# A planned instruction order, a new load order and a relay by TensorE in a two-layer attention and FFN kernel on one core

## Chip, core and metric

The kernel runs on one core of a Trainium2 chip. The metric is the device time of one execution in microseconds (us). The kernel before takes 599.5 us (median of three runs, 598.34 to 600.8). Engines are named TensorE (PE in the profile, its weight loads PEld), VectorE (DVE), ScalarE (ACT), GpSimd (POOL) and SyncE (SP).

## The reference, cut to what matters

```python
def reference(x, wq, wk, wv, wo, beta, w1, w2):     # x [1, 2048, 640] bf16, 32 heads of 20, Dff 1728
    for _ in range(2):
        x = x + A(layernorm(x), wq, wk, wv, wo, beta)
        x = x + relu(layernorm(x) @ w1) @ w2
    return x
# A: four segments of 512 tokens. In each: causal softmax attention inside the segment, plus a read of a
# memory M (phi(q) @ M / (phi(q) @ z)); the two are mixed by sigmoid(beta); then M and z take in phi(k), v.
```

Two layers of four segments are eight pieces of work. Segments within a layer depend on each other only through the memory, and the FFN of a segment needs that segment alone. So the work of different segments may be interleaved freely.

## The kernel before

All instructions come from Python generators ("streams": scores, apply, key and query projection, relay, FFN and so on). A list scheduler walks through them with modelled durations, and each time it picks the operation that can start first; ties go to the lower "due". The picked order is then fixed on each engine, with semaphores between engines.

```python
key = (round(rank), st[2].due, n)                  # earliest start, then due, then stream number
...
each(relay, "relay", -1.9, -1.8, 8)                # dues set by hand: segment number + an offset
each(out_proj, "oproj", -0.9, -0.8, 48)
each(ffn, "ffn", 1.4, 2.4, 220)
```

Scores are made in 160 rounds, 20 per segment. A round fills two pairs of PSUM banks with scores of four heads side by side (four row groups of the array), ScalarE takes two exponentials of 128x1024 from them, GpSimd masks. Each group of heads is then applied to the values in four column groups. In segment 0 the two pairs of banks are worked separately ("half-banks").

Heads have 20 columns, and 32 heads do not fit evenly into blocks of 128. The projections give five blocks; the rest sits in spare lanes and is brought to its place (`kqL`, groups 5 to 7) by a "relay" through DRAM, eight transfers per segment:

```python
def relay(a, s):
    ...
    for r in range(4):     # kqA -> scr (DRAM), one semaphore each
        ... dma("sp", scw_sem[z][r], 122880, f, ev)
    for r in range(4):     # scr (DRAM) -> kqL
        ... dma("sp", scr_sem[r], 122880, f, [wr[r]])
```

The loads at the start:

```python
def loads_sp():
    for i in (0, 2): yield from x0("sp", i)
    yield from ld("sp", "wk", 819200, ...)
    yield from ld("sp", "wq", 819200, ...)
    yield from ld("sp", "wv", 819200, ...)
def loads_act():
    for i in (1, 3): yield from x0("act", i)
    tb = yield dma("act", sem_("d_beta"), 16384, ...)   # beta to all 128 partitions
```

Where the plan sees a gap on TensorE, it puts useless 128-column matmuls of the identity into it ("fillers").

The softmax here doesn't subtract the row's maximum and nothing guards it: scores larger than these inputs give would overflow.

Of the kernel before, what the change touches and what calls it, by code (L numbers as in the profile page):

```python
# [1 line left out]

# [3 lines left out]
dt = mybir.dt  # L6
# [5 lines left out]
H = 32  # L12
# [145 lines left out]
HOT = 1.0  # L158

# [10 lines left out]
class Sched:  # L170
    def __init__(self, prog):
        self.P = prog
        self.free = {e: 0.0 for e in ENGS}
        self.t = {}
        self.events = {}
        self.streams = []
        self.dma_free = 0.0
        self.mode = "full"
        self.log = []
        self.now = -1.0  # L180
        self.fill = None
# [16 lines left out]
    def add(self, gen, name):  # L198
        self.streams.append([0, gen, None, None, False, name])
# [8 lines left out]
    def _settle(self, st):  # L208
        while not st[4]:
            if st[2] is None:  # L210
                try:
                    y = next(st[1]) if st[3] is None else st[1].send(st[3][0])
                except StopIteration:
                    st[4] = True
                    return False
                st[3] = None
                st[2] = y
            y = st[2]
            if isinstance(y, Op):
                return True  # L220
            if y.key not in self.events:
                return False
            st[2], st[3] = None, (self.events[y.key],)
        return False
# [38 lines left out]
    def _filled(self, start, mode):  # L263
# [17 lines left out]
        self.log.append(("pe", free, end, "fill", [], tk, n))  # L281
        self.mode = "full"

    def run(self):
        while True:
# [18 lines left out]
            for n, st in enumerate(self.streams):  # L304
# [6 lines left out]
                key = (round(rank), st[2].due, n)  # L311
# [43 lines left out]
            self.log.append((e, start, end, st[5], waits, out, len(fns)))  # L355
            st[2], st[3] = None, ((out, *got) if got else out,)

# [47 lines left out]
def bass_interleave_layers__memory_aug_infini_attn__dense_activation_relu__prompt_kernel(  # L405
    nc, A_x, A_wq, A_wk, A_wv, A_wo, A_beta, B_x, B_w1, B_w2, out,
):
    with contextlib.ExitStack() as es:
        sb = lambda name, shape, dtype=dt.bfloat16: es.enter_context(nc.sbuf_tensor(name, shape, dtype))
        sem_ = lambda name: es.enter_context(nc.semaphore(name))  # L410
        P = Prog({e: sem_("clk_" + e) for e in ["act", "dve", "pool", "pe"]})
        S = Sched(P)
# [6 lines left out]
        HALVES = (0,)  # L419
        NXT, NXN, NET = 3, 2, 2  # L420
# [50 lines left out]
        X = [Slot(ps[:, 0:2, :], "SX")]  # L471
        Y = [Slot(ps[:, 2:4, :], "SY")]
        OD = [Slot(ps[:, 4, :], "OD")]
        MISC = [Slot(ps[:, 5 + k, :], "misc%d" % k) for k in range(3)]
        XNT = [[Slot(k, "xnT") for k in range(2)], [Slot(2, "xnT")]]
        XN = [Slot(xn_tok[:, k], "xn") for k in range(NXN)]
        ST6 = [Slot(stats6[:, k], "st6") for k in range(4)]
        KQA = [[Slot(kqA[b][:, :, c], "kqA") for c in range(5)] for b in range(3)]
        KQL = [Slot(kqL, "kqL")]
        SCR = [[Slot(b, "scr")] for b in range(2)]  # L480
        VA = [[Slot(v_aug[k], "va")] for k in range(3)]
        PTS = [[Slot(PT[:, k], "pt")] for k in range(2)]
        PHQ = [Slot(phq, "phq")]
        KTK = [Slot(ktok, "ktok")]
        ET = [Slot(etmp[:, k], "et") for k in range(NET)]
        BDS = [[Slot(BD[:, 4 * h:4 * h + 4], "bd")] for h in range(2)]
        OSB = [[Slot(o_sb[:, k], "osb")] for k in range(2)]
        ORAW = [Slot(oraw[:, k], "oraw") for k in range(2)]
        OTOK = [Slot(k, "otok") for k in range(2)]
        RDEN = [Slot(rden[:, k], "rden") for k in range(2)]  # L490
        RMEM = [Slot(rmem[:, k], "rmem") for k in range(2)]
        OT = [Slot(oT[:, k], "oT") for k in range(2)]
        HT = [Slot(hT, "hT")]
        xnt_sem = [[sem_("xt%d_%d" % (k, i)) for i in range(NJ)] for k in range(NXT)]
        scw_sem = [[sem_("sw%d_%d" % (b, r)) for r in range(4)] for b in range(2)]
        scr_sem = [sem_("sr%d" % r) for r in range(4)]
        ktk_sem = [sem_("kt%d" % k) for k in range(3)]
        tok_sem = [sem_("tk%d" % k) for k in range(2)]
        ot_sem = [sem_("ot%d" % k) for k in range(2)]
        dout = [sem_("do%d" % k) for k in range(4)]  # L500

        def room(a, s):
            k = a * NSEG + s
            return 0 if k == 0 else 1 + (k - 1) % 2

        def kq(b, g, n):
            return kqA[b][:, n, g, :] if g < 5 else kqL[:, n, g - 5, :]

        def bf(bank):
            return bank.bitcast(dt.bfloat16)  # L510
# [3 lines left out]
        def ld(e, name, nbytes, fn, key, waits=(), issue=700.0):  # L514
            tk = yield dma(e, sem_("d_" + name), nbytes, fn, waits, issue=issue, rate=250.0)
            S.set(*key, v=[tk])
            return tk

        xs = A_x[0].rearrange("(t p) d -> p t d", p=128)

        def w_src(w):
            return w.rearrange("(c p) d -> p c d", p=128)

        def x0(e, i):
            yield from ld(e, "x0%d" % i, 163840, lambda e: e.dma_start(x_sb[:, i, :], xs[:, i, :]), ("x", 0, i))

        def loads_sp():
            for i in (0, 2):
                yield from x0("sp", i)
            yield from ld("sp", "wk", 819200, lambda e: e.dma_start(raw[0], w_src(A_wk)), ("wkr",))  # L530
            yield from ld("sp", "wq", 819200, lambda e: e.dma_start(raw[1], w_src(A_wq)), ("wqr",))
            yield from ld("sp", "wv", 819200, lambda e: e.dma_start(wv_r[:], w_src(A_wv)), ("wv",))

        def loads_act():
            for i in (1, 3):
                yield from x0("act", i)
            tb = yield dma("act", sem_("d_beta"), 16384, lambda e: e.dma_start(
                beta_bc[:], bass.AP(tensor=A_beta.tensor, offset=A_beta.offset, ap=[[0, 128], [1, H]])), lat=4000.0)
            S.set("beta", v=[tb])

        def loads_pool():
            def late(name, nbytes, fn, waits):
                tk = yield dma("pool", sem_("d_" + name), nbytes, fn, waits, issue=1100.0, rate=250.0,
                               lat=1700.0 + nbytes / 250.0)
                return tk

            def x(s, w):
                tk = yield from late("xs%d" % s, 655360, lambda e: e.dma_start(
                    x_sb[:, 4 * s:4 * s + 4, :], xs[:, 4 * s:4 * s + 4, :]), w)
                for i in range(4):  # L550
                    S.set("x", s, i, v=[tk])
                return [tk]

            w = yield Need("wv")
            w = yield from x(1, w)
            w = yield from x(2, w)
            w = yield from late("wo", 819200, lambda e: e.dma_start(wo_r[:], w_src(A_wo)), w)
            w = [w]
            S.set("wo", v=w)
            z1 = yield Need("z1")  # L560
            got = []
            for k in range(FC):
                tk = yield from late("w1%d" % k, 442368, lambda e, k=k: e.dma_start(
                    w1_r[:, k, 0:DFF], B_w1[128 * k:128 * k + 128, :]), z1 + w)
                got.append(tk)
                w = [tk]
            S.set("w1", v=got)
            w = yield from x(3, w)
            hold = KQA[0] + VA[0]
            yield Op([("pool", 0.0, 0.0, lambda: [])], [], hold=hold)  # L570
            w = w + [t for s in hold for t in s.old]
            got = []
            for k in range(4):
                c0, c1 = (0, 4, 8, 11, 13)[k], (0, 4, 8, 11, 13)[k + 1]
                tk = yield from late("w2%d" % k, 163840 * (c1 - c0), lambda e, c0=c0, c1=c1: e.dma_start(
                    w2_r[:, c0:c1, :], B_w2[128 * c0:128 * c1, :].rearrange("(c p) d -> p c d", p=128)), w)
                got.append(tk)
                w = [tk]
            tk = yield from late("w24", 81920, lambda e: e.dma_start(
                w2_r[0:DFF - NFULL * 128, NFULL, :], B_w2[NFULL * 128:DFF, :]), w)  # L580
            S.set("w2", v=got + [tk])

        def permute():
            got = []

            def part(n, c, src, w):
                dst = (wk_p, wq_p)[n][:, :, c * 128:(c + 1) * 128].rearrange("p k (r d) -> p k r d", r=4)
                tks = []
                for d0, d1, s0 in ((0, 20, 20 * c), (20, 32, 100 + 12 * c)):
                    o, i, m = dst[:, :, :, d0:d1], src[:, :, :, s0:s0 + d1 - d0], 20 * (d1 - d0)  # L590
# [11 lines left out]
            for c in range(FC):  # L602
                for n in range(2):
                    S.spawn(part(n, c, *ws[n]), "perm")
# [804 lines left out]
```

## Time and profile before

| | before |
|---|---|
| time, median | 599.5 us |
| span of the profiled run | 595.8 us |
| TensorE busy | 574.2 us, 96% |
| VectorE, ScalarE, GpSimd busy | 421.5, 429.1, 220.2 us |
| first scores | 19.9 us |
| round 20, round 40 of scores | 72.0, 124.6 us |
| last matmul ends | 593.0 us |

The lines are shown in the prediction below. TensorE's busy share hides gaps (the 512-column matmuls of L778 are recorded with 0.38 us each, though 13 in a row take 2.81 us, 0.216 each), so starts must be compared. I call **work** the sum of all matmuls at the start-to-start times that the prediction reads from the trace (a quarter for each of four side by side), plus 0.10 us for each change between the full array and the row or column groups. What the elapsed time has beyond it I call **holes**: waits, half clock (stretches in which the trace shows half the TensorE clock granted: 0.50 from 106.1 to 112.9 us in the kernel before) and smaller losses. The trace is cut at the last score matmuls of every ten rounds (called round 10, round 20 and so on), and for each piece both numbers are read. That shows where holes lie, which a share over the whole span does not.

### The profile page before, as it was taken

The page shows a single profiled execution, that of the slowest core. Times are in us where ns is not written, and L with a number is a line of the kernel's source. Part 1 is how long each engine was busy: PE and PEld are TensorE (multiplying, and loading weights), DVE is VectorE, ACT ScalarE, POOL GpSimd, SP SyncE. Part 2 cuts the span into 40 slices and gives each one's busy share as a digit, 9 for nine tenths or more (in the row PEclk, how much of TensorE's full clock was granted, in tenths as well). Part 3 has the DMA queues.
Part 4 walks back from the last instruction along what each step waited for, and adds up shares of the span by engine and source line. Part 5 has one row for each costly group of instructions (what it writes and reads, how often), then busy time and mean ns, then how long its engine had stood idle before and what let it go on. Part 6 is the DMA issues. An engine that isn't in the chain of part 4 may idle for free.

```text
span 595.8 us, 12451 instructions
## 1 busy us (share of the span) xinstructions
PE 574.2 (96%) x5099; PEld 298.8 (50%) x5099; DVE 421.5 (71%) x998; ACT 429.1 (72%) x523; POOL 220.2 (37%) x345
## 2 busy tenths in 40 slices
PE   8999998889999999999999999999999999999998
PEld 4444444334555444554444554455544654655655
DVE  5687579998799955999575971699828796744202
ACT  4879998899897998968786876979677687223140
POOL 5563545654353533435332440344322343002000
PEclk9999999799999999999999999999999999999999
DMA  6369743656818423146227521645304641522201
GB/s 210 96 140 181 143 105 48 157 109 125 95 18 137 86 53 61 31 100 119 52 49 102 73 47 21 70 91 111 72 1 70 119 101 20 102 67 23 67 0 45
DMA packets 127657, 49.42 MB, mean 83 GB/s; under 512 B 114144, under 2 KB 126304, under 8 KB 127600
## 3 DMA queue, kind: packets, MB, share of 16 engines
q1 hardware_dynamic: 125648, 41.08, 39.1%
q0 software_dynamic: 1520, 7.21, 4.2%
q8 instruction: 40, 0.66, 0.5%
q10 hardware_dynamic: 432, 0.34, 0.2%
q14 instruction: 17, 0.14, 0.1%
HBM read 14.26 MB, written 6.55 MB: 35 GB/s over the span
## 4 chain that ended last, share of the span: by engine, by line
PE 69%; DVE 15%; ACT 8%; DMA 5%; POOL 1%; issue 1%; SPq 0%; DVEq 0%
PE ps L1302 15%; PE ps L1322 15%; PE ps L778 13%; PE ps L1041 7%; PE ps L812 6%; PE ps L1254 6%; ACT PT L1055 5%; PE ps L1123 5%; DMA otok<-oraw 2%; DMA wb<-in_A_wk_dram 1%; DVE xn_tok L726 1%; DVE x_sb L1196 1%; DVE hT L1285 1%; DVE o_sb L980 1%; DVE otok L1167 1%; DVE ktok L897 1%
## 5 line engine op out<-in xcount | busy, mean ns | idle before, releaser
L1055 ACT ACTIVATE PT<-ps 128x1024 bf16<-128x1024 f32 x256 | 247.4, 1026 | 44.7 <-PE ps L1041 44.2
L1031 POOL TENSOR_SCALAR_AFFINE_SELECT PT<-PT 128x512 bf16<-128x512 bf16 x256 | 174.3, 698 | 271.0 <-ACT PT L1055 224.4
L1302 PE MATMUL ps<-xnT,wb 128*128 128x512 bf16 x560 | 134.8, 381 | 0.1
L1322 PE MATMUL ps<-wb,hT 128*128 128x320 bf16 x896 | 131.8, 299 | 2.8 <-ACT hT L1286 1.8
L1322 PEld LDWEIGHTS ps<-wb,hT 128*128 128x128 bf16 x896 | 83.4, 98 | 41.1 <-issue 5.8
L1196 DVE TENSOR_TENSOR x_sb<-x_sb,ps 128x320 bf16<-128x320 bf16 x128 | 60.8, 479 | 59.7 <-PE ps L1322 44.8
L1302 PEld LDWEIGHTS ps<-xnT,wb 128*128 128x128 bf16 x560 | 51.2, 98 | 60.6 <-issue 8.4
L1286 ACT ACTIVATE hT<-ps 128x512 bf16<-128x512 f32 x63 | 37.7, 601 | 56.3 <-PE ps L1302 56.2
L1052 ACT ACTIVATE PT<-ps 128x1024 bf16<-128x1024 f32 x64 | 62.0, 1022 | 19.8 <-PE ps L1041 19.5
L812 PE MATMUL ps<-wv_r,xnT 128*128 128x320 bf16 x320 | 68.8, 300 | 0.0
L778 PE MATMUL ps<-xnT,wk_p 128*128 128x512 bf16 x200 | 58.0, 380 | 0.4 <-DVE kq L765 0.4
L778 PE MATMUL ps<-xnT,wq_p 128*128 128x512 bf16 x200 | 57.2, 380 | 0.1
L1254 PE MATMUL ps<-wo_r,oT 128*128 128x320 bf16 x320 | 51.1, 300 | 2.7 <-DVE oT L1218 0.9
L765 DVE CAST kq<-ps 128x512 bf16<-128x512 f32 x41 | 28.1, 688 | 35.7 <-PE ps L778 35.4
L812 PEld LDWEIGHTS ps<-wv_r,xnT 128*128 128x128 bf16 x320 | 30.1, 98 | 23.6 <-issue 5.7
L1123 PE MATMUL ps<-PT,va 128*32 128x128 bf16 (+3 forms) x896 | 41.3, 305 | 0.0
L1254 PEld LDWEIGHTS ps<-wo_r,oT 128*128 128x128 bf16 x320 | 28.8, 98 | 21.0 <-issue 5.2
L1285 DVE TENSOR_SCALAR hT<-ps 128x512 bf16<-128x512 f32 x49 | 33.3, 679 | 8.1 <-PE ps L1302 7.9
L1041 PE MATMUL ps<-kq 20*128 20x512 bf16 (+3 forms) x560 | 35.3, 301 | 3.4 <-ACT PT L1055 2.3
L726 DVE TENSOR_SCALAR xn_tok<-x_sb,mv,rstd 128x640 bf16<-128x640 bf16 x64 | 34.5, 552 | 4.4 <-POOL rstd L722 3.2
L713 DVE BATCH_NORM_STATS2 stats<-x_sb 128x6 f32<-128x320 bf16 x64 | 29.4, 461 | 2.9 <-DMA x_sb<-in_A_x_dram 2.7
L714 DVE BATCH_NORM_STATS2 stats<-x_sb 128x6 f32<-128x320 bf16 x64 | 30.2, 471 | 0.0
(95 smaller groups left out, 603.0 us busy)
## 6 DMA issues: line engine op xcount, KB each, us to landing
kqL<-kq_scr SPq DMA_DIRECT2D x32, 120.0 KB
kq_scr<-kq SPq DMA_DIRECT2D x28, 120.0 KB
out_dram<-x_sb SPq DMA_DIRECT2D x16, 160.0 KB, 1.9
wb<-in_B_w_dram POOLq DMA_DIRECT2D x5, 432.0 KB, 4.7
x_sb<-in_A_x_dram POOLq DMA_DIRECT2D x3, 640.0 KB, 4.8
wb<-in_B_w_dram POOLq DMA_DIRECT2D x2, 640.0 KB, 4.9
xnT<-xn_tok SPq DMA_TRANSPOSE x52, 2.7
wb<-in_A_wk_dram SPq DMA_DIRECT2D x1, 800.0 KB, 8.4
```

Source lines behind the costliest of these rows:

```text
L726: tn, bx = yield dve(D, 4, lambda e, a, t=t: e.tensor_scalar(a, x_sb[:, t, :], mv[:, t, 0:1], rstd[:, t:t + 1], ALU.subtract, ALU.mult), [ ...
L778: fn = lambda e, bank, k=k, w_p=w_p, c=c: e.matmul(bank, w_p[:, k, c * 128:(c + 1) * 128], xnT[:, k_, :, k, :], start=(k == 0), stop=(k == ...
L812: fn = lambda e, bank, k=k, i=i, hf=hf: e.matmul(bank[:, 0:320], xnT[:, k_, i, k, :], wv_r[:, k, hf * 320:(hf + 1) * 320], start=(k == 0), ...
L1031: tm = yield pool(590.0, lambda e: e.affine_select(out=reg, in_=reg, pattern=[[0, 4], [1, 128]], compare_op=ALU.is_ge, fill=0.0, base=0, c ...
L1041: fns.append((lambda e, x=x, j=j, hh=hh, N=N, o=o: e.matmul(ps[:, hh, o:o + N], kq(b, gg[x], 0)[32 * hh:32 * hh + DH, 128 * j:128 * j + 12 ...
L1052: fn = lambda e: e.activation(PT[:, :, 2 * k:2 * k + 2, 1024:1280], bs.ap.rearrange("p h (x t) -> p x h t", x=2), ACT.Exp, scale=SCALE)
L1055: fn = lambda e: e.activation(PT[:, items[0], 2 * k:2 * k + 2, c0:c0 + 512], bs.ap, ACT.Exp, scale=SCALE)
L1123: return [(lambda e, hh=hh, j=j: e.matmul(bank[32 * hh:32 * hh + 32, 128 * j:L], v_flat[b][:, (j * H + 8 * hh + g) * E1:(j * H + 8 * hh + ...
L1196: ta = yield dve(320, 1, lambda e: e.tensor_tensor(xa, xa, bk.ap[:, 0:320], ALU.add), [tk], early=HOT)
L1254: fn = lambda e, bank, k=k, hf=hf, o=ot.ap: e.matmul(bank[:, 0:320], o[:, k, :], wo_r[:, k, hf * 320:(hf + 1) * 320], start=(k == 0), stop ...
L1302: fn = lambda e, bank, k=k, dc=dc: e.matmul(bank, w1_r[:, k, dc * 128:(dc + 1) * 128], xnT[:, k_, :, k, :], start=(k == 0), stop=(k == FC ...
L1322: fn = lambda e, bank, dc=dc, i=i, hf=hf: e.matmul(bank[:, 0:320], hTv[:, dc, i * 128:(i + 1) * 128], w2_r[:, dc, hf * 320:(hf + 1) * 320] ...
```

## The change

The intent is threefold. The order is planned in 20 passes: after each pass a backward sweep over the finished plan computes how late each operation could start, and these times are the dues of the next pass; the best pass is kept. wv is loaded ahead of wk and wq, since value projections need no permuted weights, and beta comes last. The first relay is done on TensorE: the identity's columns, copied into seven selection matrices, move the spare lanes to their place.

```diff
+def justify(S, dues, n):          # backward sweep: latest start of each op that keeps the end
+    ...                           # consumers + semaphore time, stream order, engine order
-            key = (round(rank), st[2].due, n)
+            key = (round(max(rank, self.free[e] + WIN[e])), st[2].due, n)      # WIN is 0 for all
...
-            yield from ld("sp", "wv", 819200, ...)          # after wk and wq
+            yield from ld("sp", "wv", 819200, ...)          # before wk and wq
...
+                w = yield Need("wqr")
                 tb = yield dma("act", sem_("d_beta"), 16384, ..., w, lat=4000.0)
...
+            def relay_pe(a, s):                             # only for the first segment of all
+                tz = yield dve(128 * len(pieces), 4, lambda e: e.memset(sel, 0.0))
+                for i, (m, c, d0, d1) in enumerate(pieces): # 7 column copies of the identity
+                    tk = yield dve(4 * (d1 - d0), 1, lambda e, ...: e.tensor_copy(...))
+                for m in range(3):
+                    for n in range(2):                      # keys, queries: 14 matmuls of 512 columns
+                        ... e.matmul(bank, sel[:, i], kqA[b][:, n, c, :], start=..., stop=...)
+                        S.spawn(out(m, n, bk, tk), "relay") # evacuation to kqL
...
-        each(relay, "relay", -1.9, -1.8, 8)
+            each(relay, "relay", -1.9, -1.8, 8, FIRST)      # hand dues of pass 0: first segment ahead
...
+        for n in range(PLANS):                              # PLANS = 20
+            P, S = plan(dues)
+            end = max(S.t.values())
+            if best is None or end < best[0]:
+                best = (end, P, S)
+            dues = justify(S, dues, n)
```

Cut: the bookkeeping of operation keys, the waits of the values for the ones columns that stand beside them (now only their readers wait), the model's constants for the first loads. The hand-set dues of pass 0 are not quite those of before: for the first segment the relay, the turning of its outputs, the output projection and the second layernorm are set 10 lower.

## The prediction

> **What bounds the kernel now.** I read the page first (busy shares, then the slices), then the windows by stage, the start in the timeline, and the chain of waits where the windows showed a hole. From the page:
>
> ```profile
> PE 574.2 (96%) x5099; PEld 298.8 (50%) x5099; DVE 421.5 (71%) x998; ACT 429.1 (72%) x523; POOL 220.2 (37%) x345
> ...
> PEclk9999999799999999999999999999999999999999
> ...
> PE 69%; DVE 15%; ACT 8%; DMA 5%; POOL 1%; issue 1%; SPq 0%; DVEq 0%
> ```
>
> TensorE is busy 96% of the span and carries 69% of the last chain, so the end is set by TensorE's work plus its holes. But its busy time is too kind: matmul records overlap. Starts give the true cost. In the timeline, a run of 13 512-column projections takes 2.81 us (0.216 each), ten 320-column ones 1.36 us (0.136 each); one 84-column matmul takes about 0.037, one 128-column 0.056; and a change between the full array and the four-row-group scores or the four-column-group applications adds 0.10 us: a lone value matmul before scores holds TensorE 0.23 instead of 0.136.
>
> I multiplied these into the instruction order of the kernel before: 960 x 0.216 + 1536 x 0.136 + 384 x 0.037 + 157 x 0.056 + 68 for scores and applications (160 rounds and 64 groups, four matmuls side by side) + 415 mode changes x 0.10 = about 552 us with the 14 warm-up matmuls. The last matmul ends at 593, so **about 41 us are holes**: that is all an order can win. Where they are, by windows (columns: length, then busy time of PE, PEld, DVE, ACT, POOL; clock; DMA share; GB/s):
>
> ```profile
> 44.00:72.00 28.00, 27.89 (x242) 11.86 (x242) 18.87 (x35) 25.93 (x32) 12.94 (x22) 1.00 0.80 152
> 72.00:97.00 25.00, 22.61 (x235) 10.89 (x232) 19.16 (x45) 22.57 (x27) 12.38 (x18) 1.00 0.59 115
> 97.00:125.00 28.00, 23.62 (x255) 10.92 (x256) 27.32 (x70) 24.74 (x29) 18.22 (x30) 0.88 0.52 115
> 125.00:153.00 28.00, 27.02 (x247) 11.54 (x243) 24.51 (x49) 25.49 (x30) 12.77 (x19) 1.00 0.56 106
> ...
> 500.00:594.00 94.00, 92.05 (x628) 56.12 (x620) 37.23 (x100) 24.60 (x41) 5.79 (x12) 1.00 0.22 47
> ```
>
> From 72 to 125 us TensorE is only 85 to 90% busy: there VectorE (27.3 of 28 us) and ScalarE are as full as it, and in the same window the granted clock falls (0.88). From 500 us on it runs alone and nearly without holes. In the hole the chain of waits goes through the exponentials in pairs, 2.4 to 2.8 us a round though two exponentials take only 1.9: the next scores need both banks, then a mode change.
>
> ```profile
> 90.63 1.84 ACT PT L1055 x2
> 92.47 0.05 issue
> 92.51 0.45 PE ps L1041 x8
> 92.96 1.93 ACT PT L1052 x2
> 94.89 0.05 issue
> 94.94 0.45 PE ps L1041 x4
> 95.39 1.92 ACT PT L1055 x2
> ```
>
> The start (timeline of TensorE): nothing useful before 12.5 us, with fillers (L622).
>
> ```profile
> 11.12 0.45 PE L690 MATMUL ps<-ident,xn_tok 128*128 128x128 bf16 x5 [1.69 <-DVE xn_tok L726]
> 11.41 1.28 PE L622 MATMUL ps<-ident 128*128 128x128 bf16 x20
> 12.53 1.24 PE L778 MATMUL ps<-xnT,wk_p 128*128 128x512 bf16 x5
> ```
>
> [...]the clock is halved in one stretch of 6.8 us, about 104 to 111 us, inside the thinnest window; that costs about 3.4 us.[...]the first relay's eight transfers through DRAM[...] queue on SyncE behind other issues (writes from 35 us, reads issued at 45.7, first use 56.8).
>
> **The change part by part.**
> 1. *Loads.* Issue to landing was 8.4, 10.1 and 11.6 us from 1.7, 2.2 and 2.8, so the three weight slots land near 10.1, 12.3 and 14.4. They now hold wv, wk, wq. The listing puts 18 value matmuls (2.4 us) between the first transposes and the first key matmul and drops 27 fillers (1.5 us). But keys wait for wk at 12.3 plus 0.5 of permuting, queries for wq at 14.4 plus 0.5: K at 12.9 to 14.0, a hole to 15.0, Q, K, Q, then three more key matmuls: 15.0 + 3.2 + 0.9 = first scores at 19.1 against 19.9. Win: 0.7 us, and 0.7 us of value work done ahead: about 1.5.
> 2. *Relay by TensorE.* Adds 14 matmuls of 512 columns (3.0 us) and, on VectorE and ScalarE, a clear, seven copies and six evacuations (about 5 us beside other work); removes eight transfers. The before-kernel never waits for that relay visibly, because the rounds had not come to it. It is needed so that rounds 12 to 20 may come early.
> 3. *Order.* Total issue work is then 552 + 3.0 - 1.5 + 13 more mode changes x 0.10 = 554.7. So the change raises the bound by 2.8 us and can win only by removing holes. I cut both listings at every tenth round of scores. Work of TensorE before / after in us, rounds 0-10: 21.4/19.5; 10-20: 25.5/17.5; 20-30: 22.2/25.8; 30-40: 19.0/22.5; actual time before: 24.5, 27.7, 25.5, 27.1. In the first twenty rounds (half-banks, whose two halves also cost TensorE some 2 us more per ten) ScalarE now has 22.2 and 20.2 us (20 exponentials x 0.915, plus the other instructions listed between them), so I give these 23.5 and 21.5; then 27.8 and 26.5, since ten paired rounds hold at least 24.5 plus a part of ScalarE's other work. Round 40 comes at 19.2 + 23.5 + 21.5 + 27.8 + 26.5 = 118.5, not 124.6: 6.1 us earlier. But by then 3.6 us less TensorE work is done (98.6 against 102.2). **Net 2.5 us** of the early holes and of the half clock.
> 4. *The rest.* 456.1 us of work are left, against 449.7 with 18.6 us of holes before. If holes stay: 118.5 + 456.1 + 18.6 = 593.2, nothing won. Ten-round stretches where TensorE has under 27 us are limited by the paired rounds to about 27.3; before had five such after round 40, after has three or four: 1 to 3 us. The others are waits over 0.15 us (12.8 of the 18.6): score to FFN, memory read for its phi, second FFN half for the last relu. Dues that know the distance to the end should help those, but many come from transfers and evacuations later than planned, which no plan sees. I take 3 to 4 us: last matmul at 589.5, time 3.5 earlier, plus something for a better draw than my floors: 594.
>
> **The rivals.**
> - *The plan closes most holes.* If half the 25 us of real waits goes, less 2.8 of new work: about 589; two thirds: 585. For it: holes are 41 us against 552, and the old priorities were ordinals by stage, not distances to the end. Against: holes are spread thin, about 1.4 us per 28.
> - *VectorE takes over as the bound.* Its work from rounds 20 to 30 grows from 18.3 to 29.3 us by the listing, more than the stretch lasts. Then TensorE waits there for evacuations, and the win of the first twenty rounds is handed back: 598 to 600.
> - *Merely moved slack.* ScalarE limits rounds 10 to 20, TensorE idles there and the half clock comes at another place: 600 to 602.
> - *The head is hidden.* The wait for wq turns the gain of part 1 to nothing: 1.5 us worse than my number.
>
> **Range and chances.** Centre 594.0 us: 599.5 less 2.5 less 3 to 4, rounded up for the gain in part 1 already counted. Low 586 is the first rival with half to two thirds of the waits gone; high 602 is moved slack. Faster by over 2% needs under 587.5, 12 us of 41 us of holes after paying 2.8: 0.20. Slower by over 2% would need new holes of 12 us in a plan that picks its best pass: 0.03. Same: 0.77.
>
> **What would show it.** First value matmul near 10.2, first key near 12.9, first scores near 19.1; exponentials of rounds 10 to 20 back to back and TensorE under 92% busy there; round 20 near 64 us; windows of 27 to 28 us per ten rounds from round 20 on; the half-clock stretch gone or moved; 14 new matmuls with 3 us; last 94 us as before. The prediction is wrong if the windows after 125 us show TensorE with clearly fewer holes than 1.4 us in 28 (then it is faster), or if VectorE is full between 64 and 95 us and TensorE waits for it (then there is no gain).

## The result and the profile after

The changed kernel takes **590.66 us** (median of four, 589.81 to 592.7) against 598.92 (four runs of the kernel before). The ratio is **0.9868** (95% interval 0.9826 to 0.9909). Ratios are the mean time of one kernel's fast runs over that of the other's in the same rounds, so not quite the ratio of the medians. A second measurement in five rounds gave 590.77 us and 0.9846 (0.983 to 0.9862). The kernel is faster by 1.3 to 1.5%: inside the stated range, within the 2% called "same", below the stated centre of 594.

The page of the profiled run (592.7 us, the slowest of its four):

```profile
PE 575.2 (97%) x5086; PEld 297.3 (50%) x5086; DVE 425.9 (72%) x1018; ACT 427.3 (72%) x520; POOL 215.5 (36%) x342
...
PEclk9979999999999999999999999999999999999999
...
PE 76%; DVE 13%; ACT 6%; DMA 3%; issue 1%; POOL 0%; SPq 0%
```

TensorE has 1 us more busy time in 5 us less span, and its share of the last chain rises from 69 to 76%. The slice with the low clock is now the third, not the eighth.

Windows by stage (length, then busy time of PE, PEld, DVE, ACT, POOL; clock; DMA share; GB/s):

```profile
44.00:72.00 28.00, 27.59 (x254) 10.18 (x256) 23.32 (x48) 27.06 (x31) 16.88 (x27) 1.00 0.53 107
72.00:97.00 25.00, 24.25 (x238) 11.63 (x228) 19.09 (x38) 23.20 (x30) 11.12 (x17) 1.00 0.71 127
97.00:125.00 28.00, 26.53 (x283) 12.88 (x280) 27.68 (x73) 26.15 (x32) 18.00 (x29) 1.00 0.55 88
125.00:153.00 28.00, 26.63 (x247) 11.99 (x248) 26.93 (x60) 23.74 (x27) 12.05 (x18) 1.00 0.71 144
...
500.00:588.00 88.00, 88.00 (x596) 54.62 (x594) 32.52 (x87) 19.70 (x33) 4.57 (x10) 1.00 0.22 47
```

The hole from 72 to 125 us has shrunk: TensorE 24.25 of 25 and 26.53 of 28 instead of 22.61 and 23.62. From 44 to 72 us ScalarE is busy 27.06 of 28 instead of 25.93. The chain of waits there consisted of exponentials before; now other TensorE work lies between the rounds (output projection L1418, key projection L878):

```profile
101.48 1.08 PE ps L878 x5
102.56 0.68 PE ps L1418 x5
103.24 0.38 PE ps L1205 x4
103.62 1.93 ACT PT L1219 x2
```

The start (timeline of TensorE; L912 are the values, L790 the transposes, L878 the keys):

```profile
9.00 0.57 PE L912 MATMUL ps<-wv_r,xnT 128*128 128x320 bf16 x3
9.41 0.44 PE L790 MATMUL ps<-ident,xn_tok 128*128 128x128 bf16 x5
...
12.22 0.58 PE L912 MATMUL ps<-wv_r,xnT 128*128 128x320 bf16 x3 [0.44 <-DVE wb L900]
12.63 1.24 PE L878 MATMUL ps<-xnT,wk_p 128*128 128x512 bf16 x5
```

The two traces cut at the rounds of scores (us; the estimate is the prediction's):

| point | before | after, estimated | after, measured | work up to there, before / after |
|---|---|---|---|---|
| first scores | 19.9 | 19.2 | 18.0 | 14.0 / 13.1 |
| round 10 | 44.4 | 42.7 | 45.3 | 35.5 / 32.8 |
| round 20 | 72.0 | 64.2 | 64.9 | 61.0 / 50.3 |
| round 30 | 97.5 | 92.0 | 92.9 | 83.2 / 76.1 |
| round 40 | 124.6 | 118.5 | 118.2 | 102.2 / 98.6 |
| last matmul | 593.0 | 589.5 | 588.1 | 551.9 / 554.7 |

Work is up by 2.8 us, holes are down from 41.1 to 33.4: from 22.4 to 19.6 up to round 40, and from 18.7 to 13.9 after it. That is the 4.9 us between the two last matmuls.

### The profile page after: what moved, and what is told of

Its sections match the earlier page's. It is cut to its first block, busy times and chain, and to the rows that moved or that the text cites.

```text
span 591.0 us, 12433 instructions
## 1 busy us (share of the span) xinstructions
PE 575.2 (97%) x5086; PEld 297.3 (50%) x5086; DVE 425.9 (72%) x1018; ACT 427.3 (72%) x520; POOL 215.5 (36%) x342
## 4 chain that ended last, share of the span: by engine, by line
PE 76%; DVE 13%; ACT 6%; DMA 3%; issue 1%; POOL 0%; SPq 0%
PE ps L1486 20%; PE ps L1466 16%; PE ps L878 13%; PE ps L1418 7%; PE ps L1205 7%; PE ps L1287 6%; PE ps L912 5%; ACT PT L1219 4%; DMA wb<-in_A_wk_dram 2%; DVE hT L1449 1%; ACT PT L1216 1%; DVE xn_tok L826 1%; DVE o_sb L1336 1%; PE ps L1155 1%; DMA oT<-o_sb 1%; DVE o_sb L1144 1%
## 5 line engine op out<-in xcount | busy, mean ns | idle before, releaser
L1195 POOL TENSOR_SCALAR_AFFINE_SELECT PT<-PT 128x512 bf16<-128x512 bf16 x256 | 172.2, 689 | 266.3 <-ACT PT L1219 220.1
L1450 ACT ACTIVATE hT<-ps 128x512 bf16<-128x512 f32 x54 | 32.3, 598 | 56.8 <-PE ps L1466 56.5
L1216 ACT ACTIVATE PT<-ps 128x1024 bf16<-128x1024 f32 x64 | 62.2, 1028 | 10.9 <-PE ps L1205 10.7
L912 PE MATMUL ps<-wv_r,xnT 128*128 128x320 bf16 x320 | 60.3, 300 | 1.5 <-DVE va L900 0.6
L865 DVE CAST kq<-ps 128x512 bf16<-128x512 f32 x44 | 30.1, 686 | 36.4 <-PE ps L878 36.4
L878 PE MATMUL ps<-xnT,wk_p 128*128 128x512 bf16 x200 | 55.3, 381 | 0.0
L878 PE MATMUL ps<-xnT,wq_p 128*128 128x512 bf16 x200 | 54.8, 386 | 0.1
L1418 PE MATMUL ps<-wo_r,oT 128*128 128x320 bf16 x320 | 52.6, 300 | 1.2 <-DMA oT<-o_sb 0.9
L1449 DVE TENSOR_SCALAR hT<-ps 128x512 bf16<-128x512 f32 x58 | 39.4, 681 | 8.2 <-PE ps L1466 7.7
L912 PEld LDWEIGHTS ps<-wv_r,xnT 128*128 128x128 bf16 x320 | 29.6, 98 | 23.0 <-issue 3.9
L826 DVE TENSOR_SCALAR xn_tok<-x_sb,mv,rstd 128x640 bf16<-128x640 bf16 x64 | 37.0, 590 | 4.8 <-DMA xnT<-xn_tok 3.6
L1418 PEld LDWEIGHTS ps<-wo_r,oT 128*128 128x128 bf16 x320 | 29.7, 98 | 18.6 <-issue 3.8
L813 DVE BATCH_NORM_STATS2 stats<-x_sb 128x6 f32<-128x320 bf16 x64 | 29.7, 465 | 2.8 <-DMA x_sb<-in_A_x_dram 2.5
L1287 PEld LDWEIGHTS ps<-PT,va 128*32 128x32 bf16 x896 | 18.9, 96 | 23.7 <-issue 11.2
```

What stands on the lines that cost most here:

```text
L878: fn = lambda e, bank, k=k, w_p=w_p, c=c: e.matmul(bank, w_p[:, k, c * 128:(c + 1) * 128], xnT[:, k_, :, k, :], start=(k == 0), stop=(k == ...
L912: fn = lambda e, bank, k=k, i=i, hf=hf: e.matmul(bank[:, 0:320], xnT[:, k_, i, k, :], wv_r[:, k, hf * 320:(hf + 1) * 320], start=(k == 0), ...
L1195: tm = yield pool(590.0, lambda e: e.affine_select(out=reg, in_=reg, pattern=[[0, 4], [1, 128]], compare_op=ALU.is_ge, fill=0.0, base=0, c ...
L1216: fn = lambda e: e.activation(PT[:, :, 2 * k:2 * k + 2, 1024:1280], bs.ap.rearrange("p h (x t) -> p x h t", x=2), ACT.Exp, scale=SCALE)
L1287: return [(lambda e, hh=hh, j=j: e.matmul(bank[32 * hh:32 * hh + 32, 128 * j:L], v_flat[b][:, (j * H + 8 * hh + g) * E1:(j * H + 8 * hh + ...
L1418: fn = lambda e, bank, k=k, hf=hf, o=ot.ap: e.matmul(bank[:, 0:320], o[:, k, :], wo_r[:, k, hf * 320:(hf + 1) * 320], start=(k == 0), stop ...
```

## The experiments

Twelve runs are all correct; one of them (e9) is the changed kernel again. "Holes" and "rounds" are from one profiled run each; times and ratios from five rounds. The change's three parts make a table; the two runs of the changed kernel are in the last row:

| 20 passes | TensorE relay | new loads | label | ratio to before | round 20 | holes to round 40 / after |
|---|---|---|---|---|---|---|
| no | no | no | before | 1 | 72.0 | 22.4 / 18.7 |
| no | no | yes | e3_loads_only | 0.9995 | 71.3 | 22.0 / 21.5 |
| yes | no | no | e5_plan_only | 0.9994 | 72.7 | 27.3 / 17.8 |
| no | yes | yes | e1_plans1 | 0.9995 | 69.3 | 17.7 / 22.6 |
| yes | no | yes | e2_dma_relay | 0.9973 | 72.5 | 23.4 / 14.4 |
| yes | yes | no | e6_plan_and_relay | 0.9878 | 66.6 | 18.5 / 16.5 |
| yes | yes | yes | changed kernel | 0.9868, 0.9846 | 64.9, 64.3 | 19.6 / 13.9, 19.0 / 13.7 |

Half-clock stretches are inside these holes: up to round 40 about 6.8 us in the kernel before, e3, e6 and both profiles of the changed kernel, 13.7 in e2 and e5, none in e1. At the 0.50 granted in it, a stretch costs at most half its length. e1 (one pass) uses the changed pass-0 dues, and e5 and e6 keep the changed kernel's other small edits, so a row is a part of the change as nearly as the code allows.

### e1_plans1: relay and loads without the planning

```diff
-PLANS = 20
+PLANS = 1
```

> The changed kernel with one planning pass instead of 20: new loads and TensorE relay stay, priorities are the old hand-set stages. Theory (the backward-pass dues close the holes after the start): holes after round 40 go back from 13.8 us to about 18, the early stretch 0 to 40 also loses; time about 598 to 601 us, ratio to before 1.00 +- 0.005. Rival (the gain comes from the loads and the relay, any order will do): time within 2 us of the changed kernel, 589 to 593, ratio 0.987.

Measured: 598.69 us (597.34 to 600.52), ratio 0.9995 (0.9971 to 1.002). Holes up to round 40 were fewer than in the changed kernel (17.7), but after it they were 22.6 us, more than the 18 expected. So the theory holds for the late part. For the early part it misses as the numbers stand; but this profile has no half clock, and the changed kernel without its own (at most 3.4 us) would have about 16.2, so that part is not settled. At a clock of 1.0, four spans of e1 are 595.6 to 597.2 us and two of the changed kernel 588.1 and 588.7: at equal clock the planning is worth about 8 us here.

### e2_dma_relay: planning and loads, relay through DRAM

```diff
-        RELAY_PE = (0,)
+        RELAY_PE = ()
```

> The changed kernel planned anew in 20 passes with the first relay through DRAM again. Theory (the relay lets rounds 12 to 20 run early, worth more than the 3.0 us of TensorE work it costs): rounds 10 to 20 take 24 us or more instead of 19.7, round 20 after 68 us instead of 64.9, time 593 to 597. Rival (the relay was not a limit, so its 14 matmuls are a loss): time 587 to 589, 2 to 3 us better than the changed kernel.

Measured: 597.4 us (595.16 to 599.44), ratio 0.9973 (0.9947 to 1.0). Rounds 10 to 20 took 26.3 us against 19.7, round 20 came at 72.5. The time is just above the range that the theory gave; the rival is out. In the timeline of TensorE the plan itself had nothing to do in rounds 30 to 40 and put in fillers (L722), and still real waits followed:

```profile
103.86 1.46 PE L722 MATMUL ps<-ident 128*128 128x128 bf16 x23
...
105.63 0.62 PE L722 MATMUL ps<-ident 128*128 128x128 bf16 x8
106.84 0.64 PE L1155 MATMUL ps<-BD,phq 128*128 128x84 bf16 x12 [0.59 <-DVE phq L1125]
...
108.51 0.45 PE L790 MATMUL ps<-ident,xn_tok 128*128 128x128 bf16 x5 [0.39 <-DVE o_sb L1144]
```

Why is there nothing to do here? Not because the first FFN comes later: its first matmul starts at 111.6 us before, at 118.1 in e2 and at 113.6 in the changed kernel. What differs in the timelines is when the stock of other work ran out. The last key or query projection of the first three segments starts at 86.3 us before and at 91.4 in e2, but at 108.6 in the changed kernel; the last value projection at 87.1, 89.3 and 109.6. While the relay through DRAM held back rounds 10 to 20, TensorE spent these projections there (25.5 us of work in these rounds before, 23.7 in e2, 17.4 in the changed kernel), and from about 90 us until the FFN little was left. With the relay on TensorE the scores run ahead and the projections are kept for that stretch.

### e3_loads_only: the loads in the kernel before

```diff
# in the kernel before
+            yield from ld("sp", "wv", ...)        # ahead of wk, wq
-            yield from ld("sp", "wv", ...)        # behind them
+            w = yield Need("wqr")                 # beta behind wq
-                VA[b][0].drop(t, tv0[b])
+                S.set("one", b, v=[t, tv0[b]])    # only the values' readers wait for the ones columns
```

> The kernel before with the new load order alone (wv, wk, wq, beta last, and values no longer wait for the ones columns), hand-set priorities. My prediction's part 1 gave 1.5 us; the profile of the changed kernel shows first scores 1.9 us earlier, so theory: 596 to 598, ratio 0.995 to 0.998, first scores at about 18 us. Rival (the start is hidden behind later holes): ratio 1.000 +- 0.002.

Measured: 599.27 us (597.47 to 600.05), ratio 0.9995 (0.9972 to 1.0018). First scores came at 17.6 us, 2.3 earlier, yet the last matmul ended at 594.8 against 593.0: round 40 came 1.8 us later with 2.2 us more work done, and after it the holes were 21.5 us against 18.7. The rival holds. An earlier start alone was worth nothing under hand-set dues.

### e4_old_weights: changed kernel, every engine's order kept, weights issued as before

```diff
+        q = P.ops["sp"]      # after planning: put the issues of wv, wk, wq into the order wk, wq, wv
```

> The changed kernel with its instruction order kept on every engine, only the three weight loads issued in the old order (wk, wq, wv). The first value matmul must wait for wv, some 3.5 us longer (12.6 against 9.0 us). Theory (the start is on the path that sets the end, since TensorE is full nearly to the end): first scores 3 to 3.5 us later, about 21.3, and the end 2.5 to 3.5 us later: 593 to 594.5. Rival (holes later absorb it, ScalarE having slack in rounds 0 to 20): end within 1 us of the changed kernel.

Measured: 595.27 us (591.96 to 597.11), ratio 0.9932 (0.9901 to 0.9962). First scores at 22.2 us, 4.2 later than in the profile of the changed kernel; last matmul at 590.7, 2.6 later; the median is 4.6 us up. The timeline shows the wait:

```profile
12.54 0.96 PE L912 MATMUL ps<-wv_r,xnT 128*128 128x320 bf16 x3 [4.07 <-DMA wv_r<-in_A_wv_dram]
```

So in this order the start does lie on the path to the end: of the 4.2 us of delay, 2.6 us are left at the last matmul of the profile. (Not all of the 4.2 is waiting: the first value matmul came 3.5 us later, and a half-clock stretch from 11.9 to 15.4 us set in near the end of the wait; the three value matmuls above take 0.96 us, in the changed kernel 0.57.) The median lies just above the range of the theory. That it was worth nothing in e3 does not contradict this: there the order itself was another one.

### e5_plan_only: planning alone

```diff
# changed kernel with the load order of before, and
-        RELAY_PE = (0,)
+        RELAY_PE = ()
```

> The 20 planning passes alone: old load order and the first relay through DRAM. From the four runs so far, holes after round 40 were 18.7 to 22.6 us with hand-set priorities and 13.8 to 14.3 us with planned ones. Theory (planned dues cut the late holes, but without the TensorE relay the hole of rounds 30 to 40 stays): holes after round 40 about 14 us, those of rounds 30 to 40 at 6 us or more, time 596 to 599. Rival (the plan does everything): 590 to 593.

Measured: 598.28 us (597.0 to 604.06), ratio 0.9994 (0.9958 to 1.003), as the theory said in time, with 8.9 us of holes in rounds 30 to 40. The late holes were 17.8 us, more than expected; 1.7 of them are a half-clock stretch near 394 us.

### e6_plan_and_relay: planning and relay, old loads

```diff
# changed kernel with the load order of before: wk, wq, wv, beta at the front
```

> Planned in 20 passes, first relay by TensorE, old load order. Theory (relay and plan make the gain together, the loads about 2 us of it, as the plan can shape the start for itself): round 20 near 67 us, late holes about 14 us, time 592 to 594. Rival (loads are needed as well, as the fixed order with old weights lost 4.6 us): 595 or more.

Measured: 592.53 us (591.71 to 594.92), ratio 0.9878 (0.9857 to 0.9899), as the theory said. In this profile the first scores came as late as 23.3 us, and still round 20 came at 66.6. The late holes were 16.5 us, more than the 14 expected; up to 1.7 of them are a half-clock stretch near 323 us. Of the gain of 1.3 to 1.5%, planning and relay together bring 1.2%. At a clock of 0.994, four spans of e6 are 590.0 to 591.7 us and three of the changed kernel 590.0 to 591.0, so at equal clock the new loads add at most about 1 us to a newly planned order.

### e8_beta_early: changed kernel, order kept, only beta's load moved to the front

```diff
+        q = P.ops["act"]     # after planning: the issue of beta becomes the third entry again
```

> The changed kernel, same order on all engines, only the load of beta (8 KB in small pieces) issued second on ScalarE's queue again, ahead of the weights. wv landed 8.9 us in, 1.2 us earlier than the first weight did before, though it sits in the same place of the queue. Theory (beta's small pieces took the time): first value matmul at about 10.2 instead of 9.0, first scores 1 us later, end 0.5 to 1.2 us later. Rival (beta cost nothing, the landing time is scatter): no difference, first value matmul at 9.0 +- 0.3.

Measured: 593.5 us (589.98 to 594.1), ratio 0.9884 (0.9861 to 0.9908). The first value matmul came at 12.33 us, not 9.0, first scores at 22.3, not 18.0. The bandwidth in 40 slices of the first 24 us, first of the changed kernel, then of this run:

```profile
GB/s 0 0 0 109 290 361 382 363 354 356 346 346 384 382 386 371 363 265 68 36 26 2 0 0 2 38 107 242 427 273 44 0 0 0 0 0 0 77 43 256
```

```profile
GB/s 0 0 0 196 322 333 329 230 162 187 155 162 126 230 308 333 357 393 393 335 198 139 98 98 70 36 13 0 0 0 111 85 273 435 188 27 0 0 0 0
```

With beta at the front the rate falls to 126 to 230 GB/s between 4 and 8 us. It is a transfer of 8 KB to 128 partitions. Issue to landing of the three weights was 10.5, 12.1, 13.6 us here against 7.2, 8.9, 10.4; and it is not scatter: with beta in front the third weight took 11.6 to 13.6 us in six profiles, with beta behind 8.8 to 10.7 in eight. But of 4.3 us at the first scores only 1.4 us were left at the last matmul (589.5 against 588.1; the changed kernel has a half-clock stretch in rounds 0 to 10 there and this run has none, which hides up to 3.4 us more; this run has one of 3.4 us from 13.0 us, right after the wait). The median is 2.8 us up, across two calls; taken as ratios to the kernel before of each call the difference is 0.2 to 0.4%, and the intervals touch. At a clock of 0.997 four spans are 590.8 to 592.4 us against 588.5 to 589.0, but the one execution at 1.0 took 588.2, as the changed kernel does. So how much of the 2.8 us is the late landing and how much the half clock after it stays open.

### e9_after_again and e10_old_weights_beta_late

The first is the changed kernel as it is; the second:

```diff
# changed kernel, planned anew: weights wk, wq, wv
-                w = yield Need("wqr")
+                w = yield Need("wv")          # beta behind all three
```

> The changed kernel once more, in five rounds beside the others and the kernel before. Its first four runs had mean clocks of 0.994 to 1.0 against 0.988 to 0.994 of the kernel before. Theory (8 us are some 5 us of order and some 3 us of less half clock): ratio 0.986 to 0.990, mean clock 0.996 to 0.998. Rival (the first four were a lucky draw of clocks): mean clock 0.992 and ratio 0.990 to 0.993.

> Planned in 20 passes with the TensorE relay, weights in the old order (wk, wq, wv), but beta still last, behind all of them. Beta first gave last weights at 11.6 to 13.6 us in five runs, beta last 8.8 to 10.4 us in five. Theory (of the load change only beta's place counts): first scores at 17 to 18.5 us, time within 2 us of the changed kernel's in this call. Rival (wv first is what counts, as values can run while keys are permuted): first scores 2 us or more later, time 2 us or more above the changed kernel.

Measured: the changed kernel 590.77 us, ratio 0.9846 (0.983 to 0.9862), mean clock 0.9964 against 0.9911 for the kernel before. The other 596.78 us (594.57 to 600.57), ratio 0.9952 (0.992 to 0.9984), with first scores at 21.5 us: the theory that only beta's place counts is out for the first scores. But the times don't give the worth of wv's place. e6 has the same weight order and beta in front, landings up to 1.4 us later, and is 4 us faster. Each planning anew gives another order all through, and these two differ by 4 us without a cause that the runs show. This touches the relay too: at a clock of 1.0, three spans of e10 are 592.8 to 593.2 us, and the one of e2, planned without the TensorE relay, is 593.4. So an order with the relay can end as late as one without; what the five orders with the relay share (changed, e1, e6, e10, e12) is that rounds 10 to 20 take 19.7 to 21.9 us, against 24.9 to 27.7 in the four orders without (before, e2, e3, e5). Only e4 and e8, which keep the order, measure a part by itself.

### e7_stuffed and e11_stuffed_real: is the half clock made by too little work?

In the kernel before TensorE ran at half clock for 6.8 us, from 106.1 to 112.9 us (the prediction put it 2 us too early). Both kernels keep the order of before and add useless matmuls to the stretch of 80 to 106 us of the plan:

```diff
+                if STUFF[0] < start < STUFF[1] and start - self.stuffed > STUFF[2]:
+                    self._stuff()     # e7: 6 of 128 columns, identity; e11: 2 of 512 columns, real weights; ten times
```

> The kernel before, same order on all engines, with ten groups of 6 useless 128-column matmuls (3.4 us of TensorE) put into the thin stretch of 80 to 110 us. Theory (the half clock at 104 to 111 us comes from TensorE having too little to do there): mean clock rises from 0.992 to 0.996 or more, no half-clock stretch near 100 us, and the time stays within 1 us or falls by up to 2, as the added work lies in holes. Rival (the half clock has another trigger, e.g. a fixed rhythm or the transposes): clock stays at 0.991 to 0.994 and the time rises by 1 to 3 us.

> The kernel before in its own order, with ten pairs of useless 512-column matmuls on real weights (4.3 us of TensorE) in the stretch of 80 to 110 us, where ten groups of identity fillers (3.4 us) had left the half clock as it was. Theory[...]: no half-clock stretch near 100 us, mean clock 0.996 or more, time 597 to 600. Rival (too little TensorE work is not the trigger): clock 0.990 to 0.993, time 602 to 604.

Measured: 602.83 us and 1.0045 (1.0022 to 1.0068); 604.49 us and 1.0073 (1.0055 to 1.0091). The clocks, 0.9907 and 0.9915, are those of before. Both give what the rival said: the clock stays, and the times (the second just above its range) rise. The added 3.4 and 4.3 us of work cost nearly their full length (2.7 and 4.4 us of mean time). In the timeline of e7 the six groups from 94 to 107 us take 0.50 us each with no wait ahead of them, and TensorE still waits 0.96 us before the scores at 98.31 us and 1.11 before those at 109.70: they did not slip into the waits.

The profiles show why this did not settle the trigger. The stretch and the 3.4 us ahead of it (half the stretch's length), of the kernel before, of the changed kernel and of e7:

```profile
102.70:106.10 3.40, 1.39 (x36) 0.65 (x28) 3.40 (x12) 3.29 (x4) 3.12 (x6) 1.00 0.36 72
106.10:112.90 6.80, 5.78 (x47) 2.53 (x48) 6.51 (x20) 6.08 (x8) 5.00 (x11) 0.50 0.86 194
```

```profile
30.90:34.30 3.40, 1.18 (x12) 0.56 (x10) 3.40 (x9) 2.19 (x3) 3.40 (x3) 1.00 0.00 0
34.30:41.20 6.90, 6.90 (x43) 2.03 (x43) 2.77 (x12) 3.56 (x5) 1.97 (x4) 0.51 0.78 192
```

```profile
107.20:110.60 3.40, 1.79 (x40) 0.77 (x37) 3.07 (x10) 2.89 (x4) 2.63 (x6) 1.00 0.34 84
110.60:117.50 6.90, 5.47 (x46) 2.48 (x47) 6.61 (x20) 6.18 (x8) 5.10 (x11) 0.51 0.86 184
```

Each time the 3.4 us ahead of the half clock have TensorE busy for little: 1.39, 1.18 and 1.79 us. In e7 the last useless matmuls start at 105.78 us and take 0.50 us, so they ended before this thin stretch (107.2 to 110.6 us) and missed it. Elsewhere between 20 and 580 us, in steps of 0.2 us, the thinnest 3.4 us of the kernel before hold 2.02 us of TensorE (from 91.6 us), those of the changed kernel 2.16 (from 191.2 us), and the clock stays at 1.00 after both. That is a reading of traces after the fact; no run took the thin stretch away alone, so the trigger is not shown by experiment.

### e12_searched: an attempt at a better version

```diff
-HOT_NS = 0.0
-PLANS = 20
+HOT_NS = 500.0      # operations that empty PSUM, and a few more, get dues 500 ns lower
+PLANS = 60
+            dues = {k: v + _q.gauss(0, 100) for k, v in (keep if n % 3 == 2 else dues).items()}   # fixed seed
```

> An attempt at a better version: 60 planning passes with seeded noise on the dues, the best plan kept; its own plan is about 1 us shorter than the changed kernel's. Theory (the plan is followed closely, so 1 us of plan is 1 us of time): 0 to 2 us below the changed kernel of this call. Rival (what is left is not in the plan: clock, landings): no difference, within 1 us either way.

Measured: 589.78 us (589.17 to 595.34), ratio 0.9857 (0.9821 to 0.9893) against 0.9846 of the changed kernel. The profiled run, at full clock, ended its last matmul at 584.7 us with 28.6 us of holes. But two of six runs had clocks of 0.991 and 0.994 and spans of 593.6 us. There is no difference; the rival holds. (HOT_NS is a second edit that the expectation does not name.)

## Why the prediction was right, point by point

- **Bound and margin: right.** TensorE's work set the scale: it rose by 2.8 us as computed (552 to 554.7), and all gain is holes, 41.1 to 33.4.
- **Loads: right in direction, mis-sized.** The step that failed is "so the three weight slots land near 10.1, 12.3 and 14.4". It took the slots as given; they came at 8.9, 11.1 and 13.2, since beta's 8 KB no longer ran beside them (with beta in front again, e8, they came at 12.2, 14.3 and 16.4). First scores came 1.9 us earlier instead of 0.8. At the end the load change is worth, in the medians, 2.8 us for beta's place (e8) and 4.6 us for the weights' order (e4) in this one order, each with the half clock that followed the wait, and nothing alone (e3).
- **Relay: right.** It is a price of 3 us of TensorE that buys rounds 10 to 20 at ScalarE's pace: 19.7 us (ScalarE busy 19.2) instead of 27.7, and 26.3 in e2. Its sign "TensorE under 92% busy" holds for the work (17.5 of 19.7 us); the recorded busy time is full there.
- **Early holes: right in sum.** Round 40 was put at 118.5 us and came at 118.2. In detail two errors cancelled: the profiled run had a half-clock stretch from 34 to 41 us (0.51 granted), so rounds 0 to 10 took 27.3 us instead of 23.5; the start and rounds 10 to 20 were quicker than estimated. That the sum fits to 0.3 us is luck.
- **The rest: mis-sized a little.** "I take 3 to 4 us" measured 4.8 (18.7 to 13.9). By the cuts used here, stretches of ten rounds after round 40 with under 27 us of work number six before and two after, not five and "three or four". The table of experiments supports the dues as their cause: hand-set dues left 18.7 to 22.6 us of late holes in five profiles of three orders, planned ones 13.6 to 17.8 in nine.
- **Centre: not what the sum gives.** Its part 4 ends at a last matmul of 589.5 us, 3.5 earlier, which makes 596 out of 599.5. The stated 594 takes off the 2.5 us of early gain once more, though the sum had already spent it on the 2.8 us of added work, and names the rest "a better draw". Measured profile against profile, both at a clock of 0.994, the gain is 4.8 us (597.5 to 592.7). So 594 lay nearer to the result than 596 by luck.
- **Half clock: the missing term.** The prediction had one stretch, from one profile. Over eleven runs the kernel before had a mean clock of 0.9911, the changed one 0.9964 over five. (1 - clock) x span is about 5.3 and 2.1 us lost: some 3 us of the 9 between the means (600.1 and 591.0) is clock. At a clock of 0.994 the kernel before has spans of 595.2 to 598.0 us, the changed one 590.0 to 591.0; so some 6 us are order. This, with a last matmul 1.4 us earlier than forecast, fits the 5 us between 596 and the mean of 591.0. Part of the clock may come from the loads: e4, e6 and e8, with beta in front or wv last, run at half clock near 12 to 13 us (from 11.9 us in e4 and 13.0 in e8; in e6 ten transposes from 12.02 us take 1.25 us, ten at full clock in e2 0.72). From 11 to 16 us the profile of the changed kernel has a clock of 1.00; but so has the kernel before, with beta in front and wv last, and no run shows the link.
- **Rivals.** VectorE did not fill rounds 20 to 30: it was busy 19.5 of 28 us there, where the listing had 29.3. It became full later (27.68 of 28 and 26.93 of 28 us from 97 to 153), but the holes of rounds 30 to 40 beside it fell from 8.1 (half clock included) to 2.8 us, so it did not take the gain. Moved slack happened in the profiled run with the half clock, at 34 us instead of 106. The hidden head is what e3 shows for the loads alone.

What stays open: an experiment on the half clock's trigger, and how much of a difference between two planned orders is the part that was changed and how much is chance (4 us between e6 and e10, as against the 6 to 7 us by which leaving out the relay changed the medians).

## What to carry to other kernels

When one engine carries nearly all of the span, compute its bare work from start-to-start times and cut both the trace and the new order at marks of the program: the difference is what a new order can win, and it says where. A part that opens room (here the relay) and one that uses it (here the planned dues) may each measure as nothing alone and only together as a gain; so test pairs, and test a part by itself only with the order held fixed. Look at what tiny transfers run beside the first big ones: 8 KB spread to all partitions held up 2.4 MB of weights by some 3 us (issue to landing of the three from 7.2, 8.9 and 10.4 us to 10.5, 12.1 and 13.6, e8).
